# Five of 28 weight sums moved from GpSimd to VectorE, and the second half's operand loads placed behind the first query weights

## The chip, the core and the metric

The kernel runs on one core of one Trainium2 chip. The metric is device time in microseconds of one execution. Engines are called as the profile calls them: PE is TensorE (matmuls), PEld its weight load, DVE is VectorE, ACT is ScalarE, POOL is GpSimd, and SP issues most DMAs.

## What is computed

A layer norm, a linear attention block and a gated MLP over the same input, cut to what matters:

```
xn = layernorm(x)                              # x is 2048 x 1024
q, k, v = split(xn @ wqkv)                     # 32 heads of 32
pq, pk = phi(q), phi(k)                        # t > 0: t + 1, else exp(t); + 1e-6
s = ((pq @ (pk^T v)) / (pq . sum(pk) + 1e-6)) @ wo
h = silu(x @ w1) * (x @ w3)                    # 2048 x 3584; here x is xn
out = x + s * silu(h @ w2)
```


## The kernel before

**Products.** Every big product is one step of a Strassen-like scheme: seven products (B11, T2, T3, T1, B21, T4, B22) of weight combinations with seven operand combinations (A11, S2, S3, S1, A12, A22, S4). Each float32 number is split into a high and a low part, so each block is three matmuls (L103 to L105, `mm3`). A high part is an ACT cast (L95), a low part a DVE subtraction (L96), both in `split`. One product of `gemm` is twelve 128x512 matmuls.

**Halves.** The tokens go in two halves of 1024. For a half, `half(h)` holds the seven operands in SBUF (7 x 2 MB) and runs over weights of 256 columns: four pairs of keys k and queries q from wqkv, then 14 pairs of gate g and up u from w1 and w3. In the second half key and query weights alternate (k0, q0, k1, q1, ...), and k0 and q0 run side by side, product by product. After them come the row products that stand in for the values.

**Weights.** `Operands.ask` (L415 to L418) loads one raw weight of 128x8x256 (1 MB) into one of two raw buffers. It can be issued only when the weight before last has made its last split (B22). `Operands.made` then combines (DVE, L451) and splits the raw weight product by product.

**Between the halves.** The second half's operands lie in DRAM in a_d. They are loaded by 28 DMAs on SP (L813 to L815), four per operand, each as soon as the last product of the first half that reads the old operand has run. The last pair of the first half (g13, u13) also runs side by side.

**Jobs.** Work off the main path is cut in steps and put into `jobs`; `catch_up`, called after each product, runs one step of the first job. In the first half the job is `next_work`: it prepares the second half's operands, then makes 28 `weight_sums`, one for each of 14 blocks of w2 and each half of the columns. One weight sum loads 128x4x256 of w2 (two DMAs of 256 KB on SP, L900), makes four subtractions of 128x256 on POOL (`sums_of`, L886 to L890), and stores 512 KB to wt_d (SP, L907), which the last layer reads later. A job's tiles come from four buffers of `job_tile`. In a job that is in order, the step's instructions are issued behind the last `ask` (`fetched`).

**Order.** Outside a hand-written opening the framework's scheduler orders the instructions of each engine when the kernel is built; the engines then run them in that order. SP issues DMAs one after the other, over eight semaphores in turn, so at most eight are under way. What a DVE instruction waits for, all DVE instructions behind it wait for too.

Of the kernel before, what the change touches and what calls it, by code (L numbers as in the profile page):

```python
# [9 lines left out]
F32 = mybir.dt.float32  # L10
# [6 lines left out]
P = 128  # L17
# [5 lines left out]
def tile_linear_attention_times_swiglu(  # L23
# [10 lines left out]
    nc = tc.nc  # L34
    x, out = x[0], out[0]
    S, D = x.shape
    F = w1.shape[1]
    ND = D // P
    NF = F // P
# [43 lines left out]
    AOPS = ["A11", "S2", "S3", "S1", "A12", "A22", "S4"]  # L83
# [5 lines left out]
    a_d = {n: dram.tile([P, 2, ND // 2, C], F32, name=f"a_d{n}") for n in AOPS}  # L89
# [30 lines left out]
    def signed(name):  # L120
        return pc.tile([P, C], F32, tag="sg", bufs=4, name=name)

    def job_tile(shape, name):
        return praw.tile(shape, F32, tag="job", bufs=4, name=name)
# [29 lines left out]
    def operand_tiles(h):  # L154
        return {n: pa.tile([P, 2, ND // 2, C], FR, tag=n, name=f"{n}_{h}") for n in AOPS}
# [243 lines left out]
    def columns(w, c0, n):  # L399
        return w[:, c0:c0 + n].rearrange("(k p) n -> p k n", p=P)  # L400

    fetched = []

    class Operands:
# [10 lines left out]
        def ask(self):  # L415
            if self.raw is None:
                self.raw = praw.tile([P, ND, 2 * P], F32, tag="raw", name=f"w{self.name}")
                fetched[:] = [nc.sync.dma_start(out=self.raw, in_=columns(self.w, self.c0, 2 * P))]  # L418

        def upto(self, n):  # L420
            while n not in self.B:
# [98 lines left out]
    jobs = []  # L520
# [100 lines left out]
    def phi(src, dst, z=None):  # L621
        for _ in phi_steps(src, dst, z):
            pass
# [153 lines left out]
    def half(h):  # L777
        A = operand_tiles(h)

        def keys(pair, **how):  # L780
            return gemm(ops[f"k{h}_{pair}_"], A, uses[pair], **how)

        def run(g):
            for _ in g:
                pass

        def side_by_side(*gemms):
            for _ in zip_longest(*gemms):
                pass

        def queries(pair, **how):

            def use_q(n, c, src):
                j = 2 * pair + n
                pq = signed(f"pq{h}_{j}_{c}")
                phi(src, pq)
                nc.gpsimd.dma_start(out=pq_d[j // JG][2 * h + c][:, j % JG], in_=pq)  # L797

            return gemm(ops[f"q{h}_{pair}_"], A, use_q, **how)

        uses = [key_rows(h, pair) for pair in range(ND // 2)]
        if h == 0:
            early = [ops[f"k0_{pair}_"] for pair in range(ND // 2)]
            m = [keys(pair, early=True, own=pair == 0, led=pair == 0) for pair in range(ND // 2)]
            some = mybir.EngineType
            with tc.manual_schedule(engines={some.PE, some.Activation, some.DVE, some.Pool}):
                last = Opening(A, early, m).run()
            for k in early[2:]:
                k.ask()
            early[2].then = early[3].next  # L810
        else:

            for n in AOPS:  # L813
                for k in range(ND // 2):
                    nc.sync.dma_start(out=A[n][:, :, k].bitcast(F32), in_=a_d[n][:, :, k])  # L815
        if h == 0:
            with tc.issue_after(last.ins):
                for g in m:
                    run(g)
        else:  # L820
            side_by_side(keys(0, paired=True), queries(0, paired=True))
            for pair in range(1, ND // 2):
                run(keys(pair))
                run(queries(pair))
            jobs.append((all_denominators(), False))
            for _ in row_products():
                pass
        jobs.append((attention_work(), False) if h else (next_work(), True))
        if h == 0:
            for pair in range(ND // 2):  # L830
                run(queries(pair))
        for pair in range(NF // 2):
            last = h < NH - 1 and pair == NF // 2 - 1
            gemms = [gemm(ops[f"{'gu'[e]}{h}_{pair}_"], A, use, paired=last) for e, use in enumerate(hidden(h, pair))]
            if last:
                side_by_side(*gemms)
            else:
                for g in gemms:
                    run(g)
        for j, _ in jobs:  # L840
            run(j)
        jobs.clear()
# [14 lines left out]
    def hidden(h, pair):  # L857
        sg = {}
        i = [f1 > 2 * pair for f0, f1 in FB].index(True)
        k = pair - FB[i][0] // 2  # L860

        def use_gate(n, c, src):
            sg[n, c] = signed(f"sg{h}_{pair}_{n}{c}")
            nc.scalar.activation(sg[n, c], src, AF.Silu)

        def use_up(n, c, src):
            nc.vector.tensor_mul(out=sg[n, c], in0=src, in1=sg[n, c])  # L867

            src = sg[n, c].rearrange("p (g t s) -> p g t s", t=2, s=P)[:, :, 0] if n == 0 else \
                sg[n, c].rearrange("p (e s) -> p e s", s=P)  # L870
            nc.gpsimd.dma_start(out=h_d[i][2 * h + c][:, 2 * n:4 * n + 2, k], in_=src)  # L871
            if (n, c) in ((0, 1), (1, 0)):
                sums(c)

        def sums(c):
            o = [small(f"hs{h}_{pair}_{c}_{e}") for e in range(2)]
            for e, _ in enumerate(four_sums(sg[0, c], sg[1, c], *o)):
                queue = nc.gpsimd if h == 0 or pair == NF // 2 - 1 else nc.sync
                queue.dma_start(out=h_d[i][2 * h + c][:, 6 + 4 * e:10 + 4 * e, k],  # L879
                                in_=o[e].rearrange("p (e s) -> p e s", s=P))  # L880

        return use_gate, use_up

    def sums_of(b11, b12, b21, b22):

        nc.gpsimd.tensor_sub(out=b11, in0=b12, in1=b11)  # L886
        nc.gpsimd.tensor_sub(out=b12, in0=b22, in1=b12)
        yield True
        nc.gpsimd.tensor_sub(out=b22, in0=b22, in1=b11)
        nc.gpsimd.tensor_sub(out=b21, in0=b21, in1=b22)  # L890

    def weight_sums(u, half):

        cols = slice(half * 2 * P, (half + 1) * 2 * P)

        def load():
            t = job_tile([P, 4, 2 * P], f"w2_{u}_{half}")
            for e in range(2):
                f = 2 * u + e
                nc.sync.dma_start(out=t[:, 2 * e:2 * e + 2],  # L900
                                  in_=w2[f * P:(f + 1) * P, :].rearrange("p (n c) -> p n c", c=C)[:, :, cols])
            return t

        def steps(t):
            yield from sums_of(*(t[:, i] for i in range(4)))
            yield True
            nc.sync.dma_start(out=wt_d[u][:, :, cols], in_=t)  # L907
            yield True

        return Job(load, steps)  # L910

    def next_work():

        yield from go_on([prepare_next(i) for i in range(TH // 2)])
        yield from go_on([weight_sums(u, half) for u in range(NF // 2) for half in range(2)])

    hm4 = const.tile([P, P // DH], F32, name="hm4")
    nc.vector.memset(hm4, 0.0)
# [29 lines left out]
    def go_on(work, ahead=2):  # L948

        data = [j.load() for j in work[:ahead]]  # L950
        for i, j in enumerate(work):
            yield from j.steps(data[i])
            if i + ahead < len(work):
                data.append(work[i + ahead].load())
# [132 lines left out]
    def all_denominators():  # L1087
        yield from spread_z()
        yield from go_on([j for c in range(NCH) for j in denominators(c)])

    def attention_work():
        work = [divide(m, k) for m in range(2) for k in range(ND // 2)]
        for k in range(ND // 2):
            for e, j in enumerate(merge_wo(k)):
                work += key_values(k + e * (ND // 2)) + [j]
        work += [divide(m, k) for m in range(2, S // (2 * P)) for k in range(ND // 2)]
        yield from go_on(work, 3)
# [15 lines left out]
    ops = [o for g in groups for o in g]  # L1113
    for o, o.next in zip(ops, ops[1:]):
        pass
    ops = {o.name: o for o in ops}
# [156 lines left out]
    def hiddens(i, m):  # L1273
        return left(m, lambda n: h_d[i][m // NT][:, PLACE[n][m % NT]], (FB[i][1] - FB[i][0]) // 2, f"B{i}")
# [7 lines left out]
    def second_weights(i, n, k):  # L1282
        if (i, n, k) not in asked:
            ask(i, n, k, small)
        return asked[i, n, k]

    def ask_next():

        for n, place in zip(PRODUCTS, (spare, spare, small, small)):
            ask(0, n, 1, place)  # L1290
# [104 lines left out]
    def layer_place(n, i, k):  # L1395
# [4 lines left out]
                      lambda n, _, k, i=i: second_weights(i, n, k),  # L1400
                      lambda m, i=i: hiddens(i, m), lambda m, t, n: acc[m][:, t, n],
# [40 lines left out]
```

## Time and profile before

| what | value |
|---|---|
| median of 3 runs | 2333.54 us (2331.86 to 2333.63) |
| profiled execution, own time | 2329.57 us |
| its span | 2327.8 us |
| PE busy | 2288.8 us, 98% |
| DVE, ACT, POOL busy | 1773.8, 927.4, 686.7 us |
| TensorE clock granted | 0.999 |
| change of halves, last load of g13/u13 work to first keys | about 700 to 790 us from the start |

The page gives for each engine the share of the span in which it was busy. The view by windows gives the same for stretches of time; the view of waits lists who waited for whom; the timeline lists single instructions with start, duration, line, tiles, and in brackets the idle time ahead of it with what ended it. Numbers behind a tile name (wk__6262) are the builder's own and differ from build to build. `wk` and `wq` without more are raw key and query weights, `w` a weight sum's tile, and T2k is the product operand T2 of a key weight.

### The profile page before, as it was taken

Reading aid. Unit: us, or ns where it says so; the run is one execution under the profiler, and the core shown is the slowest. Engines: PE = TensorE matmul, PEld = TensorE weight load, DVE = VectorE, ACT = ScalarE, POOL = GpSimd, SP = SyncE. Lnnn points to the kernel's source line nnn. Section 1 sums busy time; section 2 is a strip of 40 time slices with the busy share of each in tenths; the row PEclk is TensorE's granted clock in tenths of the full one; section 3 lists DMA queues with packets and bytes.
Section 4 is the critical chain, followed back from the end, with each engine's and each line's share of the span. In section 5 each row is a group of like instructions: output and inputs, shape, how many; then the busy total and the mean of one; then the engine's idle time right before and its main releaser. Section 6 shows DMA issues by size and latency. Waiting matters only on the chain.

```text
span 2327.8 us, 31758 instructions
## 1 busy us (share of the span) xinstructions
PE 2288.8 (98%) x10752; PEld 1873.8 (80%) x10752; DVE 1773.8 (76%) x2820; ACT 927.4 (40%) x1645; POOL 686.7 (30%) x851
## 2 busy tenths in 40 slices
PE   6999999999999999999999999999999999999998
PEld 5888888888887888777887888888888888888876
DVE  8987888798877775657867788887655666776798
ACT  6555443433332555433333433234333624242433
POOL 3220524287766111001423334442310000000033
PEclk9999999999999999999999999999999999999999
DMA  6555556576669546786756666765755556665688
GB/s 235 163 190 176 185 164 199 163 240 199 225 223 339 199 136 213 263 253 200 228 181 188 193 200 208 208 207 176 235 179 185 183 175 187 223 205 180 193 267 261
DMA packets 353698, 478.69 MB, mean 206 GB/s; under 512 B 24208, under 2 KB 262800, under 8 KB 353424
## 3 DMA queue, kind: packets, MB, share of 16 engines
q1 hardware_dynamic: 315808, 356.58, 48.9%
q0 software_dynamic: 37728, 120.09, 15.8%
q8 instruction: 84, 1.38, 0.3%
q14 instruction: 78, 0.64, 0.1%
HBM read 305.66 MB, written 174.59 MB: 206 GB/s over the span
## 4 chain that ended last, share of the span: by engine, by line
PE 47%; issue 8%; DMA 5%; DVE 4%; POOL 3%; ACT 1%; SPq 0%; POOLq 0%; DVEq 0%; ACTq 0%
PE g L103 2%; PE g L104 2%; PE g L105 2%; PE cB L105 1%; PE dB L105 1%; PE dB L103 1%; PE dB L104 1%; PE cB L103 1%; PE cB L104 1%; PE aB L105 1%; PE aB L103 1%; PE aB L104 1%; DMA qs_d<-qd 1%; PE bB L103 1%; PE bB L105 1%
## 5 line engine op out<-in xcount | busy, mean ns | idle before, releaser
L871 POOL DMA_DIRECT2D h_d<-sg x112 | 82.9, 741 | 258.9 <-DVE sg L867 221.3
L1190 POOL DMA_DIRECT2D u_d<-uB x32 | 17.4, 542 | 402.6 <-DVE uB L1173 346.2
L96 DVE TENSOR_TENSOR xy<-xy,xy 128x512 fp32r<-128x512 f32 x112 | 73.0, 686 | 64.6 <-ACT xy L95 64.6
L95 ACT CAST xy<-xy 128x512 fp32r<-128x512 f32 x112 | 65.0, 620 | 102.1 <-PE g L105 60.6
L104 PE MATMUL g<-xy,xy 128*128 128x512 f32 x224 | 87.7, 392 | 0.5 <-DVE xy L96 0.4
L105 PE MATMUL g<-xy,xy 128*128 128x512 f32 x224 | 87.2, 390 | 0.0
L103 PE MATMUL g<-xy,xy 128*128 128x512 f32 x224 | 82.5, 397 | 0.0
L641 POOL DMA_DIRECT2D y_d<-y x48 | 34.9, 727 | 117.3 <-ACT y L665 71.0
L1173 DVE TENSOR_TENSOR acc<-cB,acc 128x512 f32<-128x512 f32 x50 | 34.4, 688 | 42.3 <-PE cB L105 42.2
L1173 DVE TENSOR_TENSOR acc<-dB,acc 128x512 f32<-128x512 f32 x56 | 38.6, 688 | 30.1 <-PE dB L105 29.9
L851 POOL TENSOR_TENSOR hs<-hs,sg 128x256 f32<-128x256 f32 x56 | 59.7, 1067 | 0.1
L853 POOL TENSOR_TENSOR hs<-sg 128x256 f32<-128x256 f32 x56 | 58.9, 1051 | 0.0
L103 PEld LDWEIGHTS g<-xy,xy 128*128 128x128 f32 x224 | 41.8, 188 | 14.0 <-issue 3.7
L1009 POOL DMA_DIRECT2D qs_d<-qd x32 | 18.1, 567 | 116.9 <-DVE qd L1005 77.5
L1304 POOL DMA_DIRECT2D s_d<-s x32 | 17.4, 543 | 118.9 <-DVE s L1173 70.1
L854 POOL TENSOR_TENSOR hs<-sg,hs 128x256 f32<-128x256 f32 x56 | 50.3, 899 | 1.5
L104 PEld LDWEIGHTS g<-xy,xy 128*128 128x128 f32 x224 | 42.0, 188 | 10.5 <-DVE xy L96 1.8
L850 POOL TENSOR_TENSOR hs<-sg,sg 128x256 f32<-128x256 f32 x56 | 49.6, 886 | 1.2
L105 PEld LDWEIGHTS g<-xy,xy 128*128 128x128 f32 x224 | 42.0, 188 | 8.9
L797 POOL DMA_DIRECT2D pq_d<-pq x32 | 17.6, 549 | 101.2 <-DVE pq L631 100.5
L879 POOL DMA_DIRECT2D h_d<-hs x60 | 46.4, 774 | 2.7 <-POOL hs L854 2.1
L95 ACT CAST XS4B<-rS4B 128x384 fp32r<-128x384 f32 (+1 forms) x40 | 19.7, 493 | 60.5 <-PE cB L105 41.1
(5325 smaller groups left out, 8287.3 us busy)
## 6 DMA issues: line engine op xcount, KB each, us to landing
h_d<-hs POOLq DMA_DIRECT2D x60, 256.0 KB, 3.5
h_d<-sg POOLq DMA_DIRECT2D x56, 256.0 KB, 4.2
w<-in_B_w SPq DMA_DIRECT2D x56, 256.0 KB
wt_d<-w SPq DMA_DIRECT2D x28, 512.0 KB
xy<-x_d SPq DMA_DIRECT2D x28, 512.0 KB
xy<-y_d SPq DMA_DIRECT2D x28, 512.0 KB
h_d<-hs SPq DMA_DIRECT2D x52, 256.0 KB
y_d<-y POOLq DMA_DIRECT2D x48, 256.0 KB, 3.8
```

The lines of the kernel that those rows point to most:

```text
L95: nc.scalar.copy(out=hi, in_=src)
L96: return nc.vector.tensor_sub(out=lo, in0=src, in1=hi.bitcast(F32))
L103: nc.tensor.matmul(acc, lhsT=wh, rhs=ah, start=start, stop=False, skip_group_check=True)
L104: nc.tensor.matmul(acc, lhsT=wh, rhs=al, start=False, stop=False, skip_group_check=True)
L105: return nc.tensor.matmul(acc, lhsT=wl, rhs=ah, start=False, stop=stop, skip_group_check=True)
L850: e.tensor_add(out=s1, in0=a21, in1=a22)
L851: e.tensor_sub(out=s2, in0=s1, in1=a11)
L853: e.tensor_sub(out=s3, in0=a11, in1=a21)
L854: e.tensor_sub(out=s4, in0=a12, in1=s2)
L871: nc.gpsimd.dma_start(out=h_d[i][2 * h + c][:, 2 * n:4 * n + 2, k], in_=src)
L879: queue.dma_start(out=h_d[i][2 * h + c][:, 6 + 4 * e:10 + 4 * e, k], in_=o[e].rearrange("p (e s) -> p e s", s=P))
L1173: return V.tensor_add(out=c, in0=src, in1=c)
```

## The change

Two edits. The 28 weight sums are listed in `WSUMS`; the first 23 stay in `next_work` on POOL, the last five are a job of their own, `last_weight_sums`, with all four subtractions on DVE. That job is put into the list in the second half behind k0 and q0, so its steps run from k1 on. And in the second half q0's raw weight is asked before the operand loop, and the operands from the third on (S3, S1, A12, A22, S4) are issued behind that load.

```
         def ask(self):
             if self.raw is None:
                 self.raw = praw.tile([P, ND, 2 * P], F32, tag="raw", name=f"w{self.name}")
-                fetched[:] = [nc.sync.dma_start(out=self.raw, in_=columns(self.w, self.c0, 2 * P))]
+                self.asked = nc.sync.dma_start(out=self.raw, in_=columns(self.w, self.c0, 2 * P))
+                fetched[:] = [self.asked]
...
-            for n in AOPS:
-                for k in range(ND // 2):
-                    nc.sync.dma_start(out=A[n][:, :, k].bitcast(F32), in_=a_d[n][:, :, k])
+            ops["q1_0_"].ask()
+            for i, n in enumerate(AOPS):
+                with ExitStack() as behind:
+                    if i > 1:
+                        behind.enter_context(tc.issue_after(ops["q1_0_"].asked.ins))
+                    for k in range(ND // 2):
+                        nc.sync.dma_start(out=A[n][:, :, k].bitcast(F32), in_=a_d[n][:, :, k])
...
             side_by_side(keys(0, paired=True), queries(0, paired=True))
+            jobs.append((last_weight_sums(), True))
...
-    def sums_of(b11, b12, b21, b22):
-
-        nc.gpsimd.tensor_sub(out=b11, in0=b12, in1=b11)
-        nc.gpsimd.tensor_sub(out=b12, in0=b22, in1=b12)
+    def sums_of(b11, b12, b21, b22, e=nc.gpsimd):
+
+        e.tensor_sub(out=b11, in0=b12, in1=b11)
+        e.tensor_sub(out=b12, in0=b22, in1=b12)
         yield True
-        nc.gpsimd.tensor_sub(out=b22, in0=b22, in1=b11)
-        nc.gpsimd.tensor_sub(out=b21, in0=b21, in1=b22)
+        e.tensor_sub(out=b22, in0=b22, in1=b11)
+        e.tensor_sub(out=b21, in0=b21, in1=b22)
...
+    WSUMS = [(u, half) for u in range(NF // 2) for half in range(2)]
+    NOW = len(WSUMS) - 5
+
     def next_work():
 
         yield from go_on([prepare_next(i) for i in range(TH // 2)])
-        yield from go_on([weight_sums(u, half) for u in range(NF // 2) for half in range(2)])
+        yield from go_on([weight_sums(*w) for w in WSUMS[:NOW]])
+
+    def last_weight_sums():
+        yield from go_on([weight_sums(*w, nc.vector) for w in WSUMS[NOW:]])
```

The order of the instructions follows at three places. The first is SP's queue at the change of halves: A11_1 to S4_1 are the second half's operands, wk1_0 and wq1_0 the raw weights of its first keys and queries, w2_ a weight sum's load, wt_d its store. Before:

```order
L815 DMA A11_1_6466<-a_dA11_172 128x2x512 x4
L815 DMA S2_1_6467<-a_dS2_173 128x2x512 x4
L418 DMA wk1_0__6262<-in_A_wqkv 128x8x256
L815 DMA S3_1_6468<-a_dS3_174 128x2x512 x4
L418 DMA wq1_0__6281<-in_A_wqkv 128x8x256
L907 DMA wt_d12_126<-w2_12_1_6171 512x1x256
L900 DMA w2_13_1_6305<-in_B_w2 128x2x256 x2
L907 DMA wt_d13_127<-w2_13_0_6239 512x1x256
L815 DMA S1_1_6469<-a_dS1_175 128x2x512 x4
```

And now, from the same operand on:

```order
L820 DMA A11_1_6426<-a_dA11_172 128x2x512 x4
L820 DMA S2_1_6427<-a_dS2_173 128x2x512 x4
L418 DMA wk1_0__6238<-in_A_wqkv 128x8x256
L418 DMA wq1_0__6255<-in_A_wqkv 128x8x256
L820 DMA S3_1_6428<-a_dS3_174 128x2x512 x4
L820 DMA S1_1_6429<-a_dS1_175 128x2x512 x4
```

The query weight has moved ahead of S3, and the two stores and one load between it and S1 are gone; a third store, behind S4, is gone too.

The second place is DVE at the same change: the low parts (L96) of the first weights' operands among the last sums of g13 and u13. Before, from B11 of q0 to T2 of k0:

```order
L96 TENSOR_TENSOR B11q1_0__6302<-wq1_0__6281,B11q1_0__6302 128x512
L617 TENSOR_TENSOR c12g0_13__6432<-dg0_13__6199,ug0_13__6153 128x512
L96 TENSOR_TENSOR T3k1_0__6327<-wk1_0__6262,T3k1_0__6327 128x512
L451 TENSOR_TENSOR wq1_0__6281<-wq1_0__6281 128x4x128
L451 TENSOR_TENSOR wk1_0__6262<-wk1_0__6262 128x4x128
L451 TENSOR_TENSOR wq1_0__6281<-wq1_0__6281 128x4x128
L617 TENSOR_TENSOR c12u0_13__6451<-du0_13__6221,uu0_13__6176 128x512
L867 TENSOR_TENSOR sg0_13_10_6434<-c12u0_13__6451,sg0_13_10_6434 128x512
L96 TENSOR_TENSOR T3q1_0__6348<-wq1_0__6281,T3q1_0__6348 128x512
L96 TENSOR_TENSOR T2k1_0__6367<-wk1_0__6262,T2k1_0__6367 128x512
```

And now:

```order
L96 TENSOR_TENSOR B11q1_0__6275<-wq1_0__6255,B11q1_0__6275 128x512
L96 TENSOR_TENSOR T3k1_0__6295<-wk1_0__6238,T3k1_0__6295 128x512
L452 TENSOR_TENSOR wq1_0__6255<-wq1_0__6255 128x4x128
L610 TENSOR_TENSOR c21g0_13__6232<-eg0_13__6182,c21g0_13__6232 128x512
L452 TENSOR_TENSOR wk1_0__6238<-wk1_0__6238 128x4x128
L452 TENSOR_TENSOR wq1_0__6255<-wq1_0__6255 128x4x128
L610 TENSOR_TENSOR c21u0_13__6252<-eu0_13__6203,c21u0_13__6252 128x512
L96 TENSOR_TENSOR T3q1_0__6314<-wq1_0__6255,T3q1_0__6314 128x512
L873 TENSOR_TENSOR sg0_13_01_6348<-c21u0_13__6252,sg0_13_01_6348 128x512
L96 TENSOR_TENSOR T2k1_0__6332<-wk1_0__6238,T2k1_0__6332 128x512
```

The same preparation now stands a product earlier: T2 of k0 came behind the last sums of u13 (c12u, which reads its last product) and now comes behind c21u, two products before that.

The third place is DVE during k1, where the first moved weight sum (w2_11_1) enters, between two PSUM reads of k1 (c21k and c22k):

```order
L587 TENSOR_TENSOR c21k1_1__6844<-ck1_1__6805,uk1_1__6774 128x512
L892 TENSOR_TENSOR w2_11_1_6824<-w2_11_1_6824 128x256
L680 SCALAR_TENSOR_TENSOR y01_1_0_6651<-trk1_0_10_6850,y01_1_0_6651 128x512
L681 SCALAR_TENSOR_TENSOR r2_1_0_6855<-trk1_0_10_6850,y10_1_0_6798 128x512
L893 TENSOR_TENSOR w2_11_1_6824<-w2_11_1_6824 128x256
L96 TENSOR_TENSOR T2q1_1__6790<-wq1_1__6574,T2q1_1__6790 128x512
L96 TENSOR_TENSOR T1q1_1__6821<-wq1_1__6574,T1q1_1__6821 128x512
L684 TENSOR_TENSOR y00_1_0_6701<-r2_1_0_6855,y00_1_0_6701 128x512
L594 TENSOR_TENSOR c22k1_1__6845<-dk1_1__6806,c21k1_1__6844 128x512
```

Before, c22k stood two rows behind c21k, with one row between them; now seven rows stand between, two of them of the weight sum. On SP the load of w2_11_1 is issued right behind the raw weight of k2, w2_12_1 behind that of q2, and w2_13_0 and w2_13_1 behind that of k3. From the row products on the order of every engine is as it was.

More of the change, by code (lines that the diff above doesn't have):

```diff
@@ L882, in hidden, with weight_sums @@
         return use_gate, use_up
-    def sums_of(b11, b12, b21, b22):
-        nc.gpsimd.tensor_sub(out=b11, in0=b12, in1=b11)
-        nc.gpsimd.tensor_sub(out=b12, in0=b22, in1=b12)
+    def sums_of(b11, b12, b21, b22, e=nc.gpsimd):
+        e.tensor_sub(out=b11, in0=b12, in1=b11)
+        e.tensor_sub(out=b12, in0=b22, in1=b12)
         yield True
-        nc.gpsimd.tensor_sub(out=b22, in0=b22, in1=b11)
-        nc.gpsimd.tensor_sub(out=b21, in0=b21, in1=b22)
-    def weight_sums(u, half):
+        e.tensor_sub(out=b22, in0=b22, in1=b11)
+        e.tensor_sub(out=b21, in0=b21, in1=b22)
+    def weight_sums(u, half, e=nc.gpsimd):
         cols = slice(half * 2 * P, (half + 1) * 2 * P)
@@ L897, in load @@
             t = job_tile([P, 4, 2 * P], f"w2_{u}_{half}")
-            for e in range(2):
-                f = 2 * u + e
-                nc.sync.dma_start(out=t[:, 2 * e:2 * e + 2],
+            for i in range(2):
+                f = 2 * u + i
+                nc.sync.dma_start(out=t[:, 2 * i:2 * i + 2],
                                   in_=w2[f * P:(f + 1) * P, :].rearrange("p (n c) -> p n c", c=C)[:, :, cols])
@@ L904, in steps @@
         def steps(t):
-            yield from sums_of(*(t[:, i] for i in range(4)))
+            yield from sums_of(*(t[:, i] for i in range(4)), e)
             yield True
```

## The prediction

> **What bounds the kernel now.** I read the page first.
>
> ```profile
> span 2327.8 us, 31758 instructions
> PE 2288.8 (98%) x10752; PEld 1873.8 (80%) x10752; DVE 1773.8 (76%) x2820; ACT 927.4 (40%) x1645; POOL 686.7 (30%) x851
> ```
>
> PE is busy for 98% of the span. The change adds and removes no matmul, so it can only move PE's pauses. The view by windows shows which lie where the change works.
>
> ```profile
> core 0: us, PE busy (x) PEld busy (x) DVE busy (x) ACT busy (x) POOL busy (x), PEclk, DMA share, GB/s
> 740.00:750.00 10.00, 8.08 (x35) 5.94 (x33) 9.91 (x9) 4.57 (x9) 7.09 (x10) 1.00 1.04 393
> 750.00:760.00 10.00, 9.91 (x44) 7.99 (x43) 9.37 (x15) 2.63 (x5) 3.40 (x4) 1.00 1.05 400
> 780.00:790.00 10.00, 8.64 (x42) 6.95 (x41) 9.08 (x17) 8.54 (x16) 3.28 (x5) 1.00 0.26 84
> 800.00:820.00 20.00, 20.00 (x98) 16.54 (x97) 16.62 (x33) 12.03 (x21) 5.86 (x9) 1.00 0.52 158
> 820.00:840.00 20.00, 20.00 (x90) 16.57 (x89) 14.63 (x26) 10.74 (x18) 1.33 (x3) 1.00 0.26 93
> 840.00:860.00 20.00, 20.00 (x97) 16.54 (x97) 15.20 (x28) 11.27 (x20) 5.93 (x9) 1.00 0.52 158
> ```
>
> PE pauses only around 740 to 751 and around 783; after 800 it is full, with DVE at 73 to 83%. The idle time is 1.92 + 0.09 + 1.36 = 3.4 us. The starts of PE's instructions give it more exactly, since a matmul's 0.39 us overlaps the next one: of the 90 in 20 us two reach over the edges, so there is one per 20 / 88 = 0.227 us (0.23 in two digits), so a product of twelve takes 2.72 us.
>
> ```profile
> 742.84 0.39 PE L105 MATMUL aq__6520<-A,B11q__6302 128*128 128x512 f32 x1
> 744.02 0.50 PE L103 MATMUL bk__6538<-S,T2k__6367 128*128 128x512 f32 x1 [0.79 <-ACT T2k__6367 L95]
> 744.35 0.40 PE L104 MATMUL bk__6538<-S,T2k__6367 128*128 128x512 f32 x1
> 745.88 0.51 PE L105 MATMUL bk__6538<-S,T2k__6367 128*128 128x512 f32 x1 [1.13 <-DVE T2k__6367 L96]
> 749.88 0.39 PE L105 MATMUL ck__6539<-S,T3k__6327 128*128 128x512 f32 x1
> 750.36 0.50 PE L105 MATMUL bq__6559<-S,T2q__6388 128*128 128x512 f32 x1
> ...
> 770.62 0.44 PE trk L637 x4
> 782.30 0.60 PE L637 MATMUL trk<-ident,pk 128*128 128x128 f32 x4
> 784.25 0.50 PE L103 MATMUL bk__6844<-S,T2k__6662 128*128 128x512 f32 x1 [1.36 <-ACT T2k__6662 L95]
> ```
>
> PE waits for T2 of k0, high part then low part, and later for T2 of k1. The lost time is 744.02 - 742.84 - 0.23 = 0.95 us ahead of the first, 745.88 - 744.35 - 0.23 = 1.3 us ahead of the second, 0.25 us ahead of the low part of T2 of q0 (750.36), and about 0.1 us more at each of these restarts (744.02 to 744.35 is 0.33): 2.8 us. At 784 it is 784.25 - 782.30 less the 0.44 of four transposes, 1.5 us, with the restart 1.6 us. **In all 4.4 us** stand within reach, 3.4 us by the windows; I take 4.4.
>
> Why is T2 of k0 late? SP, ACT and DVE answer.
>
> ```profile
> 715.45 0.37 SPq L418 DMA_DIRECT2D wk__6262<-in_A_wqkv  x1
> 716.06 6.90 SPq L815 DMA_DIRECT2D S<-a_dS  x4
> 723.05 0.56 SPq L418 DMA_DIRECT2D wq__6281<-in_A_wqkv  x1
> 758.03 1.51 SPq L418 DMA_DIRECT2D wk__6597<-in_A_wqkv  x1
> ...
> 727.00 0.62 ACT L95 CAST B11k__6283<-wk__6262 128x512 fp32r<-128x512 f32 x1 [2.13 <-DMA wk__6262<-in_A_wqkv]
> 736.23 0.62 ACT L95 CAST B11q__6302<-wq__6281 128x512 fp32r<-128x512 f32 x1 [4.64 <-DMA wq__6281<-in_A_wqkv]
> ...
> 716.72 0.99 DVE L96 TENSOR_TENSOR B22u__6259<-wu__5962,B22u__6259 128x512 fp32r<-128x512 f32 x1
> 736.88 0.70 DVE L96 TENSOR_TENSOR B11q__6302<-wq__6281,B11q__6302 128x512 fp32r<-128x512 f32 x1 [3.02 <-ACT B11q__6302 L95]
> 744.62 1.21 DVE L96 TENSOR_TENSOR T2k__6367<-wk__6262,T2k__6367 128x512 fp32r<-128x512 f32 x1
> 746.89 2.27 DVE L451 TENSOR_TENSOR wk__6262<-wk__6262 128x512 f32<-128x512 f32 x1
> ```
>
> The key weight lands by 727.0, the query weight 9.2 us later, with S3 between them. ACT and DVE run in order, and behind B11 of q0 stands the rest of k0. From 736.9 both weights' preparation has to go through a DVE that is 99% busy (9.91 of 10 us), while PE ends its first products at 743.
>
> **The query weight's move.** It may be asked once u13's raw weight is free, at 716.72 + 0.99 = 717.7; SP now reaches it at once, instead of at 723.05. The DMA view gives the sizes:
>
> ```profile
> S<-a_dS SPq DMA_DIRECT2D x16, 512.0 KB
> wq__6281<-in_A_wqkv SPq DMA_DIRECT2D x1, 1024.0 KB
> ```
>
> Between the two landings 4 x 512 + 1024 KB came in 9.2 us, 333 KB per us. The queue stays busy through the stage (0.4 MB per us in the windows), so the query weight alone lands 1024 / 333 = 3.1 us after the key weight: 730.1 instead of 736.2. The order shows ten DVE rows from B11 of q0 to T2 of k0, and the next rows give their step:
>
> ```profile
> 753.12 0.68 DVE L96 TENSOR_TENSOR B21k__6463<-wk__6262,B21k__6463 128x512 fp32r<-128x512 f32 x1
> 753.72 0.68 DVE L96 TENSOR_TENSOR B21q__6516<-wq__6281,B21q__6516 128x512 fp32r<-128x512 f32 x1
> ```
>
> Ten times 0.60 us behind the cast at 730.7 is 736.7; T2 of q0, four rows on, 739.1. PE wants them at 743.1 and 745.8. Both have over 6 us to spare, so the 2.8 us go.
>
> S3 is paid for this. It lands at 730.1 + 2048 / 333 = 736.2, and S1, A12, A22 and S4 each 6.15 us later: 742.4, 748.5, 754.7, 760.8. PE wants them, counting products of 2.72 us from 743.1, at 748.5, 753.9, 759.3, 765.3 and 768.0. The closest has 7 us. The three stores and one load of weight sums that stood among them (2 MB) no longer do; what is late next is nothing here.
>
> **k1's weight.** It is asked when k0's last split is done. That split reuses a buffer of k0's T3 product, which ends at 751.2, so about 752.5 instead of 758.03; the load lands at 760.8 + 3.1 = 763.9. In the new order T2 of k1 comes behind c12k of k0, whose product ends at 773.9 (768.0, then twelve matmuls of it, a transpose group and q0's T4 product); two DVE rows later it is 775.1. PE, 4.4 us earlier than at 784.25, wants it at 779.8. The 1.6 us go too.
>
> **The twenty subtractions.** POOL loses them, where PE waited for none. On DVE none of 128x256 with two inputs is in the trace. The nearest rows are a memset of that size and the 128x512 rows above.
>
> ```profile
> 905.12 0.27 DVE L927 MEMSET zb<- 128x256 f32 x1
> 861.41 0.46 SPq L701 DMA_DIRECT2D xy<-y_d  x1
> ```
>
> So 0.27 to 0.69 us each, 5.4 to 13.8 us; I take 0.35, half a 128x512 one, near the memset: 7 us. From 800 to 860 DVE idles 3.4 + 5.4 + 4.8 = 13.6 us while PE is full. The sums fit, at the upper end only just. I cost them at nothing, as long as none stands waiting in DVE's queue (below). On SP the first row products' second load (861.41 before) now stands behind the last store, which waits for a sum that comes just behind k3's last split; the load ahead of it waits for that same split, so the delay is under 1 us.
>
> **The sum.** -2.8 - 1.6 + 0 = -4.4 us. Against the profiled execution: 2329.57 - 4.4 = 2325.2 us (its span is 2327.8, 1.8 us less than its time). The median, 2333.54, is 4.0 us above that execution, so I carry the difference over: **2329.1 us**, -0.19%. A difference of 0.2%, 4.7 us, is about what a measurement of this kernel can tell from no change.
>
> [...] POOL runs beside the slow DVE rows:
>
> ```profile
> 738.28 1.11 POOL L886 TENSOR_TENSOR w<-w 128x256 f32<-128x256 f32 x1 [1.25 <-DMA w<-in_B_w]
> 747.85 0.74 POOL L889 TENSOR_TENSOR w<-w 128x256 f32<-128x256 f32 x1
> L850 POOL TENSOR_TENSOR hs<-sg,sg 128x256 f32<-128x256 f32 x2 | 2.0, 986 | 0.0
> ```
>
> Each DVE subtraction that overlaps POOL takes 1.21 to 2.27 us, alone 0.68. The moved sums leave this stage, but the eight hidden sums (hs) stay. [...]
>
> **Rivals.**
>
> *POOL's hidden sums still hold DVE.* Eight of about 0.9 us (the L850 pair takes 2.0) are 7.1 us. If all fell ahead of T2 of k0, it would be ready at 736.7 + 7.1 = 743.8, 0.7 us late: 2329.8 us. Against it: POOL's work of this stage reaches past 747.85 in the rows above, and only what overlaps counts.
>
> *Only the first pause goes.* The pause at k1, or one like it, remains, since ACT and DVE there hand k0's last steps to each other in a fixed order: 2333.54 - 2.8 = 2330.7 us. For it: the schedule before had just such a pause at 784, in a stage where the DMA moved only 84 GB/s. Against it: the order gives T2 of k1 4.7 us to spare.
>
> *The change does not do what it says.* The query weight's transfer shares the engines with S3 instead of going ahead of it, and lands at 736 as before: 2333.5 us. Against it: key weight and query weight landed 9.2 us apart with S3 between, as in one line.
>
> *DVE waits for w2, slower.* The first subtraction of w2_11_1 stands between c21k and c22k of k1, and its load behind k2's 1 MB. What such a load takes:
>
> ```profile
> 681.01 0.37 SPq L418 DMA_DIRECT2D wu__5962<-in_B_w  x1
> 682.15 1.39 SPq L900 DMA_DIRECT2D w<-in_B_w  x2
> 689.21 0.73 POOL L886 TENSOR_TENSOR w<-w 128x256 f32<-128x256 f32 x1 [8.78 <-DMA w<-in_B_w]
> ```
>
> 8.2 us from the weight's issue to the first sum. k1's last split is eight DVE rows behind T2 of k1, 775.1 + 4.8 = 779.9, so k2's weight is asked near 780.5, and w2_11_1 is there at 788.7. Then eight rows, three of them short, 3.7 us: c22k is read by 792.4. PE adds B22 of k1 into the same bank at 793.8 (779.8, two products, a transpose group, three products). So it decides from a landing at 790.1. At worst the weight takes 11.55 us (715.45 to 727.00) and the sum's 512 KB 1.5 us more: 793.6, c22k at 797.3, PE 3.5 us late. Three loads stand so behind a raw weight (k2, q2, k3): 10.5 - 4.4 = +6.1 us, 2339.6 us, 0.26% slower; one alone gives 2332.6. For it: only 1.4 us of slack. Against: the queue is nearly empty there (84 GB/s in 780 to 790).
>
> **How the numbers follow.** Forecast 0.57, POOL's hold 0.05, only the first pause 0.18, no effect 0.08, DVE behind w2 0.12. The sum lies 0.3 us short of the 0.2% bound, so over a third of the first two cases, with the runs' spread of 1.8 us and small pauses uncounted, may end beyond it, and a little of the third: faster by over 0.2% 0.33. Slower by over 0.2% needs several w2 waits: 0.09. The rest, 0.58, is within. The range: 1.8 us of spread below the forecast gives 2327.3, taken as 2327.0; above, it takes in the first pause alone, one w2 wait and no effect with half the spread: 2334.5.
>
> **What would show it.** Right: wq is issued near 718 and ACT's B11 of q0 starts near 730; PE's waits for T2 at 743 and near 780 are missing; PE is 10.00 of 10 us from 740 to 790. Wrong: a DVE wait on w at the first moved sum of over 4 us with a PE wait for c22k behind it; a PE wait on an operand's DMA; T2 of k1 still waited for; or DVE over 95% busy in the windows from 800 on with PE below 20.00.

## The result, and the profile after

| | before | after |
|---|---|---|
| median of 12 runs each | 2332.48 us (2329.37 to 2335.22) | 2326.57 us (2324.27 to 2331.01) |
| ratio, 95% interval | | 0.9975 [0.9968, 0.9983], 5.9 us less (4.0 to 7.5) |
| profiled execution: time, span | 2329.57, 2327.8 us | 2326.24, 2324.5 us |

Faster by 0.25%. The interval, 0.17% to 0.32%, leaves out no change; that more than 0.2% was gained is likely but not shown. The predicted 2329.1 us was 2.5 us too slow, and the median lies 0.4 us under the low end of the range (2327.0). Busy time and instructions of the engines after:

```profile
PE 2291.3 (99%) x10752; PEld 1876.9 (81%) x10752; DVE 1769.8 (76%) x2840; ACT 927.3 (40%) x1645; POOL 663.5 (29%) x831
```

The twenty subtractions show as counts alone: POOL has 20 instructions fewer, DVE 20 more. The view by windows after, in the stretches shown for before (busy time and instructions of PE, PEld, DVE, ACT, POOL, then PE's granted clock, DMA share and GB/s):

```profile
740.00:750.00 10.00, 10.00 (x45) 8.26 (x44) 10.00 (x13) 4.81 (x9) 6.58 (x9) 1.00 1.05 394
750.00:760.00 10.00, 10.00 (x46) 8.27 (x45) 5.55 (x9) 2.49 (x4) 4.72 (x6) 1.00 1.05 397
780.00:790.00 10.00, 10.00 (x50) 8.27 (x49) 9.36 (x18) 5.28 (x10) 3.46 (x6) 1.00 0.73 248
800.00:820.00 20.00, 20.00 (x95) 16.55 (x94) 17.38 (x34) 11.14 (x19) 6.25 (x10) 1.00 0.65 201
820.00:840.00 20.00, 20.00 (x92) 16.55 (x91) 16.21 (x34) 10.99 (x19) 0.93 (x2) 1.00 0.60 196
840.00:860.00 20.00, 20.00 (x96) 16.55 (x95) 16.69 (x30) 11.13 (x19) 6.31 (x10) 1.00 0.61 184
```

PE is full in all of them: 8.08, 9.91 and 8.64 us of 10 before are 10.00 now. From 800 on DVE is 0.8 + 1.6 + 1.5 = 3.8 us busier (76, 158 and 149 hundredths), and PE doesn't feel it. How T2 of k0 came in time, in the timelines of SP, ACT, DVE and PE after (start, duration, what; in brackets the idle time before it):

```profile
716.45 0.80 SPq L418 DMA_DIRECT2D wk__6238<-in_A_wqkv  x1
719.17 3.00 SPq L418 DMA_DIRECT2D wq__6255<-in_A_wqkv  x1
722.26 10.66 SPq L820 DMA_DIRECT2D S<-a_dS  x8
754.86 0.37 SPq L418 DMA_DIRECT2D wk__6557<-in_A_wqkv  x1
...
728.70 0.62 ACT L95 CAST B11k__6257<-wk__6238 128x512 fp32r<-128x512 f32 x1 [2.10 <-DMA wk__6238<-in_A_wqkv]
732.22 0.62 ACT L95 CAST B11q__6275<-wq__6255 128x512 fp32r<-128x512 f32 x1 [2.90 <-DMA wq__6255<-in_A_wqkv]
...
738.55 0.68 DVE L96 TENSOR_TENSOR T2k__6332<-wk__6238,T2k__6332 128x512 fp32r<-128x512 f32 x1
739.15 3.19 DVE L452 TENSOR_TENSOR wq__6255<-wq__6255 128x512 f32<-128x512 f32 x1
743.46 1.22 DVE L96 TENSOR_TENSOR T2q__6351<-wq__6255,T2q__6351 128x512 fp32r<-128x512 f32 x1
...
744.79 0.39 PE L103 MATMUL bk__6498<-S,T2k__6332 128*128 128x512 f32 x1
```

B11 of q0 starts 3.5 us behind B11 of k0, 9.2 us before. T2 of k0 is ready at 738.55 + 0.68 = 739.2, 5.6 us before PE takes it up at 744.79 with no idle time ahead of it. That execution was already 1.7 us late ahead of the stage (the same matmul of g13 starts at 679.51 us there and at 677.79 in the profiled before), so the spans differ by only 3.3 us.

**One number for the stage.** Below, "lost time of the stage" is the sum, from 680 to 905 us, of PE's start-to-start distances less 0.227 us per 128x512 matmul and 0.44 us per group of four transposes, the reckoning that the prediction used for its 4.4 us, but over all steps and not the pauses alone. It is 4.82 us in the profiled before and 0.27 us in the profiled after.

### The profile page after: what moved, and what is told of

Its sections match the earlier page's. It is cut to its first block, busy times and chain, and to the rows that moved or that the text cites. A ratio compares the mean times of both kernels' runs of the same rounds, so it can differ in the third digit from the quotient of the medians.

```text
span 2324.5 us, 31761 instructions
## 1 busy us (share of the span) xinstructions
PE 2291.3 (99%) x10752; PEld 1876.9 (81%) x10752; DVE 1769.8 (76%) x2840; ACT 927.3 (40%) x1645; POOL 663.5 (29%) x831
## 4 chain that ended last, share of the span: by engine, by line
PE 75%; DVE 4%; DMA 3%; issue 2%; POOL 1%; ACT 0%; SPq 0%; DVEq 0%; ACTq 0%; POOLq 0%
PE g L103 2%; PE g L104 2%; PE g L105 2%; PE cB L103 1%; PE dB L104 1%; PE cB L105 1%; PE dB L105 1%; PE dB L103 1%; PE cB L104 1%; PE aB L105 1%; PE aB L103 1%; PE aB L104 1%; PE bB L103 1%; PE bB L105 1%; PE bB L104 1%
## 5 line engine op out<-in xcount | busy, mean ns | idle before, releaser
L96 DVE TENSOR_TENSOR xy<-xy,xy 128x512 fp32r<-128x512 f32 x112 | 73.1, 686 | 64.7 <-ACT xy L95 64.5
L1185 DVE TENSOR_TENSOR acc<-cB,acc 128x512 f32<-128x512 f32 x50 | 34.4, 688 | 42.9 <-PE cB L105 42.9
```

The lines of the kernel that those rows point to most:

```text
L96: return nc.vector.tensor_sub(out=lo, in0=src, in1=hi.bitcast(F32))
L1185: return V.tensor_add(out=c, in0=src, in1=c)
```

## The experiments

Each was timed beside the kernel before, except five runs that were executed once, for a profile.

| kernel | lost time of the stage | median, before beside it | ratio, interval |
|---|---|---|---|
| before, four profiles | 4.82, 6.25, 5.22, 5.05 | | |
| the change, twice | 0.27, 0.27 | 2327.10, 2332.01 (second) | 0.9980 [0.9972, 0.9989] |
| turned loads alone | 2.56 | 2328.09, 2332.01 | 0.9985 [0.9976, 0.9994] |
| five sums alone | 1.24 | 2328.26, 2332.01 | 0.9987 [0.9978, 0.9996] |
| late sums on POOL | 0.27 | 2327.31, 2332.01 | 0.9983 [0.9974, 0.9992] |
| one sum late | 0.27 | 2326.62, 2332.45 | 0.9977 [0.9968, 0.9986] |
| three sums late | 0.27 | 2325.91, 2332.45 | 0.9976 [0.9968, 0.9985] |
| eight sums late | 0.27 | 2325.63, 2332.45 | 0.9976 [0.9967, 0.9985] |
| before, ACT's order changed | 4.69 | 2329.70, 2331.43 | 0.9995 [0.9986, 1.0004] |
| before, the first of its three edits | 6.11 | | |
| turned loads, ACT's order changed | 0.92 | 2326.39, 2331.43 | 0.9978 [0.9969, 0.9987] |
| before, pause filled, two profiles | 3.01, 2.54 | 2331.73, 2332.38 | 1.0000 [0.9991, 1.0009] |

### The change again, and its two parts

The change as it is:

> The changed kernel unaltered, timed again. If the change is worth just what the pauses of the profiled execution add up to (4.4 us), the ratio to the kernel before is near 0.9981; if it is worth more than that execution showed, it stays near the 0.9975 first measured. In the profile PE has no wait for a T2 from 740 to 790, and the first moved subtraction waits about 1 us for its load.

It gave 0.9980, 4.7 us less (2.6 to 6.5). The turned loads alone, with all 28 sums on POOL between the halves:

```
-            jobs.append((last_weight_sums(), True))
...
-    NOW = len(WSUMS) - 5
+    NOW = len(WSUMS)
```

> Only the order of the loads: all 28 weight sums stay on GpSimd, the query weight is asked ahead of S3. If the earlier query weight removes the pauses, the cast of B11 of q0 starts near 731 and 2.8 to 4.4 us go (ratio 0.9988 to 0.9981). If it is GpSimd's sums and their DMAs that held VectorE and the queue, T2 of k0 is still late and the ratio stays within 0.0004 of 1.

The five sums alone, the loads in the old order (the change's loop over AOPS taken back to the three lines of before):

> Only the sums: five go to VectorE in the second half, the loads keep their order, so S3 still lands between the key and the query weight. If the query weight's place is the cause, B11 of q0 is cast near 735 and at least 1.5 us of the 2.8 us at 743 remain, at most 2.9 us go (0.9988). If the sums are the cause, 4.4 us go (0.9981).

PE's waits from 680 to 900, of the turned loads alone and then of the sums alone (total, times, longest):

```profile
PE bk__6844 L103 <- ACT T2k__6662 L95: 1.4, 1, 1.4
PE dk__6540 L103 <- DMA S<-a_dS: 0.3, 1, 0.3
```

```profile
PE bk__6498 L105 <- DVE T2k__6332 L96: 0.6, 1, 0.6
```

The turned loads remove the first pause and leave k1's whole. They also leave a wait of 0.3 us for the last operand, S4: on SP three stores and one load of weight sums still stand ahead of it. The sums alone shrink the first pause to a wait of 0.64 us, less than the 1.5 us that was expected to stay, and remove k1's. On the way to T2 of k0 its profile differs from before in one DVE row above all: the second sum behind T3 of k0 takes 0.68 us (743.71), and took 2.25 us before (739.86), when POOL worked on a hidden sum and a weight sum beside it. k1's weight is asked at 759.29 in that run, 40.7 us behind k0's, against 42.6 before and 41.9 with the loads turned. That is 1.9 us earlier than before, so these two runs leave open whether k1's pause comes, as the prediction had it, from when that weight is asked.

The change, with the five late sums on POOL:

```
-        yield from go_on([weight_sums(*w, nc.vector) for w in WSUMS[NOW:]])
+        yield from go_on([weight_sums(*w, nc.gpsimd) for w in WSUMS[NOW:]])
```

> As the change, but the five late sums run on GpSimd instead of VectorE. If it matters only that they leave the change of halves, the time is that of the change (0.9981 to 0.9975). If the engine matters, GpSimd's twenty subtractions of about 0.9 us, each able to hold a VectorE subtraction, make VectorE late between 780 and 860: PE waits there, 0.9985 or above.

No PE wait, and a time that can't be told from the change's: which engine takes the late sums makes no difference that the runs show. That they leave the change of halves may.

### How many sums must leave

One, three and eight late sums in place of five (`NOW = len(WSUMS) - 1`, `- 3`, `- 8`). My theory by then was that k1's pause follows from PE's built order, where in the kernel before all twelve matmuls of k0 by S4 stand ahead of the first transpose of k0's rows; with one late sum that order stays.

> As the change, but only the last of the 28 weight sums is left for VectorE after k1; 27 stay on GpSimd. The built order of PE and ACT in this stage is then that of the kernel before: twelve products of k0 by S4 stand ahead of the first transpose of k0's rows. Theory O (the order on PE and ACT sets k1's pause): the first pause near 745 goes (query weight asked early), PE still waits 1.3 to 1.8 us for T2 of k1, the gap sum of the stage is 2.2 to 3.0 us, the time 2328 to 2330 us, 2 to 4 us under the kernel before. Theory W (the pause at k1 was only a matter of when GpSimd's sums and the loads leave the queues): with the loads turned, the pause at k1 is under 0.5 us and the time is that of the change, about 2327 us.

> As the change, but three sums instead of five are left for VectorE: twelve subtractions. The built order on PE and ACT is that of the change. Theory O: no pause of PE in the stage over 0.3 us, gap sum 0.2 to 0.7 us, time within 1 us of the change's (2326 to 2328 us). Rival (each sum taken from GpSimd's early stage is worth something in itself, about 5.9 / 5 = 1.2 us): 2.4 us slower than the change, 2329 us or more.

> As the change, but eight sums go to VectorE: 32 subtractions of 0.42 us, 13.4 us instead of 8.3. Theory F (free cover): VectorE idles 13.6 us from 800 to 860 in the kernel before, so even eight sums just fit; PE waits under 0.5 us in the stage, time within 1 us of the change's, 2326 to 2328 us. Rival (VectorE stands waiting for w2 loads in its queue, and PE behind it): waits for w on VectorE of over 2 us with a PE wait for a split or copy behind them, 2329 to 2333 us.

The theory fell as far as PE goes: with one late sum all twelve matmuls by S4 still stand ahead of that transpose, and k1's pause is gone all the same; that kernel is as fast as the change. (ACT's order in that build is not the old one, against what was expected; the next section takes it up.) One late sum does what five do. Three and eight gain nothing beyond that and lose nothing: 32 subtractions on DVE find room too. The longest wait of DVE for such a load in the run with eight (total, times, longest):

```profile
DVE w L892 <- DMA w<-in_B_w: 0.8, 1, 0.8
```

### What holds T2 of k1

ACT starts its rows one after the other, in the profiled before 0.46 to 0.68 us apart from T3 of k1 to T2 of k1. Its timeline there, B11 of k1 and then from T3 to T2, and in the profiled after:

```profile
775.77 0.60 ACT L95 CAST B11k__6616<-wk__6597 128x512 fp32r<-128x512 f32 x1
...
779.82 0.62 ACT L95 CAST T3k__6640<-wk__6597 128x512 fp32r<-128x512 f32 x1 [2.13 <-DVE wk__6597 L451]
780.50 0.63 ACT L627 ACTIVATE pq<-c21q__6611 128x512 f32<-128x512 f32 x1
781.04 0.62 ACT L627 ACTIVATE pk<-c12k__6777 128x512 f32<-128x512 f32 x1
781.56 0.61 ACT L627 ACTIVATE pq<-c12q__6802 128x512 f32<-128x512 f32 x1
782.08 0.61 ACT L629 ACTIVATE pq<-pq 128x512 f32<-128x512 f32 x1
782.60 0.61 ACT L629 ACTIVATE pk<-pk 128x512 f32<-128x512 f32 x1
783.12 0.56 ACT L556 COPY uk__6814<-ak__6815 128x512 f32<-128x512 f32 x1
783.58 0.62 ACT L95 CAST T2k__6662<-wk__6597 128x512 fp32r<-128x512 f32 x1
```

```profile
772.42 0.61 ACT L95 CAST T3k__6600<-wk__6557 128x512 fp32r<-128x512 f32 x1
774.78 0.63 ACT L628 ACTIVATE pq<-c21q__6571 128x512 f32<-128x512 f32 x1 [1.75 <-DVE c21q__6571 L610]
775.38 0.62 ACT L95 CAST T2k__6622<-wk__6557 128x512 fp32r<-128x512 f32 x1
...
781.31 0.59 ACT L557 COPY uk__6774<-ak__6775 128x512 f32<-128x512 f32 x1
```

Before, B11 of k1 starts without idle time ahead of it, 7.8 us before T2, so the weight had landed long before T2 was made. Six rows without a gap stand between T3 and T2, activations of k0's and q0's results and the copy of k1's own first product (uk): 3.8 us from one start to the other. After, one row does, and the copy comes 5.9 us behind T2. To see whether this place alone makes the pause, ACT's order was changed by hand in the kernel before, loads and sums untouched: B11 of k1 ahead of c21k's activations, T2 of k1 ahead of those of c21q and c12q and of uk's copy. (`first` holds the rounding instruction of each part of a weight; `issue_after` queues an engine's rows behind a given one.)

```
+            with ExitStack() as behind:
+                if (h, j, c) == (1, 0, 1):
+                    behind.enter_context(tc.issue_after(first["k1_1_", "B11"].ins))
+                yield from phi_steps(src, pk, z)
...
+                    if (h, j, c) in ((1, 0, 1), (1, 1, 0)):
+                        behind.enter_context(tc.issue_after(first["k1_1_", "T2"].ins))
+                    phi(src, pq)
...
+            if name == "k1_1_":
+                behind.enter_context(tc.issue_after(first[name, "T2"].ins))
+            copied = nc.scalar.copy(out=u, in_=ba)
```

> The kernel before, loads and all 28 sums as they were; only ScalarE's order at k1 is changed by hand: the first rounding of k1's weight stands ahead of the activations of c21k, and the rounding of T2 of k1 ahead of those of the query rows and of the copy of k1's first product. Theory Q (ScalarE's queue sets k1's pause, the weight had landed long before): the rounding of k1's first part starts at 771 to 772 instead of 775.8, PE's wait for T2 of k1 goes (under 0.3 us), the pauses for T2 of k0 and q0 stay (2.4 to 3.0 us), the time is 1 to 2 us under the kernel before. Theory L (the pause is set by when k1's weight is asked and lands): the rounding then waits for the DMA, the pause of 1.4 us stays, and the time is that of the kernel before.

The same with the first of these three edits alone, executed once:

> The kernel before with only the first rounding of k1's weight ahead of c21k's activations; the rounding of T2 of k1 stays behind the copy of k1's first product. Theory Q in its narrow form (it is T2's place behind that copy that PE waits for): the pause for T2 of k1 stays at 0.8 to 1.5 us. In its wide form (it is the first rounding's place that counts, all later ones follow): the pause goes.

And all three on top of the turned loads alone:

> As the run with the turned loads alone (28 sums on GpSimd), with the same change by hand of ScalarE's order at k1. Theory Q: no pause of PE for T2 of k0 or of k1, gap sum of the stage under 1.3 us (a wait of 0.3 us for the last x operand may stay), and the time within 1 us of the change's, 4 to 6 us under the kernel before: then the five sums on VectorE are worth nothing but the order that the build gave without them. Theory S (the sums taken from the stage are worth something in themselves): still 1 us or more slower than the change, 2328 us or more.

ACT's rows with all three edits, then with the first alone, and PE's wait in that one:

```profile
773.97 0.62 ACT L97 CAST B11k__6616<-wk__6597 128x512 fp32r<-128x512 f32 x1
784.28 0.62 ACT L97 CAST T2k__6662<-wk__6597 128x512 fp32r<-128x512 f32 x1 [1.69 <-DVE wk__6597 L454]
...
787.42 0.57 ACT L562 COPY uk__6814<-ak__6815 128x512 f32<-128x512 f32 x1
```

```profile
773.10 0.62 ACT L97 CAST B11k__6616<-wk__6597 128x512 fp32r<-128x512 f32 x1
784.64 0.56 ACT L559 COPY uk__6814<-ak__6815 128x512 f32<-128x512 f32 x1
785.11 0.62 ACT L97 CAST T2k__6662<-wk__6597 128x512 fp32r<-128x512 f32 x1
```

```profile
PE bk__6844 L105 <- ACT T2k__6662 L97: 1.4, 1, 1.4
```

B11 alone being earlier changes nothing: T2 stays behind uk, and PE waits 1.4 us as before. With T2 ahead of uk the pause is gone, with k1's weight asked at 759.22, 42.9 us behind k0's (42.6 before). So **the place of T2 of k1 in ACT's queue makes k1's pause**, not the weight. All 17 profiles split this way: in six T2 stands right behind uk's copy, and PE waits 1.36 to 1.43 us for it; in the other eleven it stands ahead of the copy, and there is no such wait. In time the three edits alone can't be told from no change (0.9995, 1.2 us less, 3.3 less to 0.9 more). On top of the turned loads they give 0.9978, 5.1 us less (3.0 to 7.2), which can't be told from the change's effect, with no sum moved; only the wait for S4 stays, 0.35 us, and the lost time is 0.92 us instead of 0.27. What the moved sums bring beside that is the order that the build gives ACT once at least one is out of the stage. What in the build decides that order wasn't found.

### How large the pauses are, and the clock behind them

The kernel before was profiled three times more.

> The kernel before once more, for a second profile. Theory: the two pauses are a matter of the built order and come back: 2.5 to 3.1 us near 745 and 1.3 to 1.8 us near 784, gap sum of the stage 4.5 to 5.5 us. Rival (the pauses differ from execution to execution, which would make the gain's size a matter of chance): one of them is off by over 1 us.

> The kernel before, a third profile. [...]

> The kernel before, a fourth profile. [...]

Both pauses came back each time: the first two waits for T2 of k0 cost 2.25 us in the first profile and 2.75, 2.61 and 2.49 in the others, k1's 1.51 or 1.52 in all four. One of the four loses clearly more than the pauses: PE's windows (busy time, instructions, granted clock, DMA share, GB/s) and two rows of its timeline in the second profile of before, then two windows in the third:

```profile
744.00:746.00 2.00, 0.78 (x3) 0.85 1.04 406
746.00:748.00 2.00, 2.00 (x5) 0.50 1.05 397
748.00:750.00 2.00, 2.00 (x9) 0.80 1.04 390
...
746.55 0.63 PE L103 MATMUL bk__6538<-S,T2k__6367 128*128 128x512 f32 x1
746.97 0.63 PE L104 MATMUL bk__6538<-S,T2k__6367 128*128 128x512 f32 x1
```

```profile
744.00:746.00 2.00, 0.73 (x2) 1.00 1.04 406
746.00:748.00 2.00, 1.17 (x5) 1.00 1.05 405
```

In the second profile the granted clock falls to 0.50 at the end of the pause, matmuls start 0.42 us apart in place of 0.23, and 2 x (0.15 + 0.50 + 0.20) = 1.7 us of clock are missing, as much as 3.4 us at 0.50 would take. In the third, with the same pauses, it doesn't fall. The time of the whole execution doesn't show the fall: 2330.92 us with it, 2329.57, 2329.58 and 2332.97 us without. To see whether PE's idling does it, ten matmuls whose sum is thrown away were put into the wait of the kernel before:

```
+        B.upto("T2")
+        for _ in range(10 if name == "k1_0_" else 0):
+            nc.tensor.matmul(bb, lhsT=B.B["B11"][:, 0, 0], rhs=A["A11"][:, 0, 0], start=True, stop=True, skip_group_check=True)
```

> The kernel before, with ten more matmuls of 128x512 (some 2.3 us, into the bank that the next product starts afresh, so that their sum is thrown away) between the first products of k0 and q0 and the product that waits for T2 of k0. The wait stays, PE is busy in it. Theory C (PE's idle time lowers its granted clock): the granted clock is 1.00 in every 2 us window from 742 to 754, the gap sum of the stage loses its 1.2 to 1.4 us of slow matmuls, time 0 to 1.5 us under the kernel before. Rival (something else lowers the clock there, the DMA at 400 GB/s for one): 0.50 to 0.87 in two or three of these windows, as without the matmuls, and the time is that of the kernel before.

> The filled kernel once more. Theory C: again 1.00 in all windows from 742 to 754. Rival: a drop to 0.50 in this or the other profile of it.

The clock stayed at 1.00 from 742 to 754 in both. That agrees with PE's idling as the cause but doesn't show it: of the six profiles with the unfilled pause (four of before, two with ACT's order changed) three have the fall and three don't, so two without it can be chance. None of the nine profiles in which this pause is gone or under 0.8 us has it. The filled kernel is no faster than before (1.0000), and it is no clean test: its build put T2 of k1 ahead of uk's copy, so k1's pause is gone too, and PE waits for T2 of q0 instead:

```profile
PE bq__6569 L105 <- DVE T2q__6388 L96: 1.4, 1, 1.4
```

Its lost time, 2.78 us on the mean of two, is 2.3 us smaller than that of the three profiles of before without a fall (5.03), 1.5 us of it k1's pause, and ten matmuls of 0.227 us take as much.

## Why the prediction was right or wrong

**The gain.** Both pauses were there in each profile, and both went. The 4.4 us were right for the profile that they were read from, which loses 4.82 - 0.27 = 4.55 us more than the change, but that profile had the shortest first pause. The four profiles of before lose 5.34 us on the mean in the stage, the two of the change 0.27: 5.1 us. The sum also left out the fall of the clock behind the pause: the one profile of four that has it lost 6.25 us, the other three 5.03. 5.1 us lies within both intervals of the change, and the mean of the seven comparisons with neither pause left is close to it, 5.2 us (5.9, 4.7, 4.0, 5.4, 5.6, 5.6, 5.1; two are the change itself). That more than the stage gained isn't shown.

**The failed step** is the sum's two inputs: the 4.4 us taken from one execution, as said, and, more so for the range, where the prediction carried the difference of 4.0 us over from the profiled execution to "the median, 2333.54", and then drew the range's low end 1.8 us under its forecast. That median stood on three runs; twelve give 2332.48, 1.06 us less. This and the gain of 5.9 for 4.4 us (1.5, of which the stage's profiles show 0.7 and the interval of 4.0 to 7.5 covers the rest) make the 2.5 us by which the forecast was off. The low end, 2.1 us under the forecast, had room for either, but not for both. So two terms were mis-sized, the time before and the gain, while which pauses go was forecast rightly. Nor is 0.2% what a measurement can just tell: the intervals here reach 0.09% to either side or less.

**The query weight's move** went as forecast. Asked at 719.17, 2.7 us behind the key weight, it was in use 3.5 us behind it (forecast 3.7), and T2 of k0 had 5.6 us to spare (forecast 6.4). Shown by the turned loads alone.

**k1's weight** was the wrong reason for a right term, and that the term came true was luck as far as the working goes. It is asked 754.86 - 716.45 = 38.4 us behind k0's (42.6 before, forecast 37.1), and T2's low part was ready at 776.48 + 0.68 = 777.2, 4.3 us before PE took it up without a wait (forecast 4.7). But with the weight asked as late as before (42.9 us behind k0's) and ACT's order changed the pause goes, and in the profiled before B11 of k1 did not wait for its load. The reverse, the weight early and ACT's order left, no run shows: the turned loads alone move it by only 0.7 us, to 41.9. The working did read the new order on DVE, where T2 of k1 stands just behind c12k, but not ACT's, which was what counted. DVE and PE after:

```profile
776.48 0.68 DVE L96 TENSOR_TENSOR T2k__6622<-wk__6557,T2k__6622 128x512 fp32r<-128x512 f32 x1
```

```profile
781.47 0.48 PE L103 MATMUL bk__6804<-S,T2k__6622 128*128 128x512 f32 x1
```

**The twenty subtractions** cost 20 x 0.42 = 8.4 us of DVE, not 7, and nothing in time. The prediction scaled its nearest row wrongly: half of the 0.68 us of a 128x512 subtraction is 0.34 us, and a 128x256 one took 0.42. Nor was such a row missing from the trace of before: low parts of 128x256 with two inputs (L96, XA11B to XS4B, eight of each) took 0.416 to 0.425 us there on the mean of each eight. The row of the profile after for the first of the four subtractions (shortest, median and longest in ns):

```profile
L892 DVE TENSOR_TENSOR w<-w x5: 415/416/424, 788.3 to 852.0; 128x256 f32<-128x256 f32 x5
```

**DVE behind w2** (the slower rival) was close, and its arithmetic held: the first sum was there at 788.3, forecast 788.7, and c22k was read at 792.92, forecast 792.4, with no PE wait behind it. DVE's waits for loads in the timeline after are these two, 1.2 us in all:

```profile
788.33 0.42 DVE L892 TENSOR_TENSOR w<-w 128x256 f32<-128x256 f32 x1 [0.39 <-DMA w<-in_B_w]
...
790.77 0.42 DVE L893 TENSOR_TENSOR w<-w 128x256 f32<-128x256 f32 x1 [0.82 <-DMA w<-in_B_w]
...
792.92 0.68 DVE L594 TENSOR_TENSOR c22k__6845<-dk__6806,c21k__6844 128x512 f32<-128x512 f32 x1
```

**POOL's hold** on DVE came harder than forecast in one place, 3.19 us for the row at 739.15, where the 128x512 subtraction ahead of it takes 0.68 us. It fell between T2 of k0 and T2 of q0, and the spare time took it.

**Only the first pause** goes with the turned loads alone, so this rival named the right danger ("ACT and DVE there hand k0's last steps to each other in a fixed order"). Only the order that came with the moved sums kept the change out of it.

## What to carry to other kernels

A wait of constant length does not tell by itself what makes it. The one for T2 of k1 was 1.36 us in five profiles and came from the order in a queue; the second one for T2 of k0 was just as constant, 1.13 or 1.14 us in six, and went when a load was moved. Look at what stands ahead of the operand's instruction on its engine, and test by moving that instruction alone. Count times from a mark in the same execution: two profiles of the kernel before differ by 1.9 us ahead of the stage (the first matmul of g13's B22 starts at 677.79 us in the first and at 679.68 in the fourth). A baseline for a gain of 0.2% wants a dozen runs and more than one profile; the first profile lost 0.2 to 1.4 us less in this stage than the next three. And when a change moves work out of a stage, try moving the least that changes the order: here one sum did what five do.

## What the runs showed of the hardware that was not expected

**The clock.** Two waits of 0.8 to 1.3 us each within 3.5 us, with two matmuls between them, were followed in three of six profiles by a granted clock of 0.50; in each of the three the windows add up to the same 1.7 us of missing clock, as much as 3.4 us at 0.50 would take. The single pause of 1.5 us at k1 was never followed by it (six profiles). Why the fall comes in some executions and not in others was not shown.

**The spread.** The clock also falls once, from some point between 2236 and 2246 us on, in eight of the 17 profiles of all these kernels, before and after alike, as in the profile after (windows of PE):

```profile
2238.00:2240.00 2.00, 1.59 (x3) 0.55 0.40 102
2240.00:2242.00 2.00, 2.00 (x7) 0.59 1.01 337
```

2 x (0.45 + 0.41) = 1.7 us of clock again. Such falls agree with a part of the 3.5 to 8.2 us by which the timed executions of one kernel differ: of the 96 of the kernel before that were timed beside the experiments, the 40 with a mean granted clock of 0.998 or more have a median of 2330.67 us, the other 56 one of 2332.92.

**POOL beside DVE.** A 128x512 subtraction of DVE took 0.68 us at 738.55 and 3.19 us at 739.15, up to 742.34. POOL's first and last hidden sum in that time, of three, in the timeline after:

```profile
739.66 0.74 POOL L856 TENSOR_TENSOR hs<-sg,sg 128x256 f32<-128x256 f32 x1
...
741.05 0.73 POOL L857 TENSOR_TENSOR hs<-hs,sg 128x256 f32<-128x256 f32 x1
```

The row took 2.5 us longer than the one ahead of it, while three in a row ran on POOL; the longest row that the prediction shows for before took 2.27 us in all. Not each DVE row that overlaps one of POOL takes longer, as the prediction had it: before, a row that began at 738.11, 0.17 us ahead of POOL's at 738.28, took 0.67 us, and POOL's took 1.11 us.
